# Filling the tile of an FFT with 8 transfers in place of 32, in a kernel that runs attention and a spectral filter side by side

## The chip, the cores and the metric

The kernel runs on one core of a Trainium2 chip. The metric is device time in microseconds, the median of several executions. One profiled execution gives the trace that the profile is read from. TensorE (PE) multiplies, VectorE (DVE), ScalarE (ACT) and GpSimd (POOL) do elementwise work, SyncE (SP) issues transfers; ScalarE and GpSimd issue transfers too, each in the order of its own instructions.

## What is computed

Two independent blocks read inputs of 2048 rows of 448 numbers, and their outputs are joined side by side.

```python
# A: attention of 16 heads of 28, one key head and one value head for all
q = (x @ wq).reshape(B, S, H, Dh).transpose(0, 2, 1, 3)
k, v = x @ wk, x @ wv
p = softmax(einsum("bhqd,bkd->bhqk", q, k) * Dh ** -0.5)
a = einsum("bhqk,bkd->bhqd", p, v).transpose(0, 2, 1, 3).reshape(B, S, H * Dh) @ wo
# B: a two-dimensional real FFT, a complex filter, the inverse
X = rfft2(x, axes=(-2, -1)) * (w_r + 1j * w_i)
b = irfft2(X, s=(S, D), axes=(-2, -1))
return concatenate([a, b], axis=-1)
```

## The kernel before

**The stages.** First come the projections of block A and, between them, the first part of block B's transform: eight loads of `xb` (q = 0 to 7) are folded on VectorE (`fft1_fold`), transformed along the row on TensorE (`fft1_a`) and along part of the column (`fft1_mm`), evicted to the tile `bs` and stored to the DRAM tensor `t1` (`fft1_out`, two stores each, L152). Load q holds the points 2q, 2q + 1, 16 + 2q and 17 + 2q of the 32 that one column index has. Load 7 is finished late, in `first_fill`, after the attention has begun.

**The tile X.** `X` has 128 partitions, 32 points, real and imaginary part, and 113 frequencies. It is filled from `t1` by transfers on GpSimd's queue (`spread`, L486); a partition's run for one point is 112 or 113 numbers. `spread(0)` takes points 0 to 7 and 16 to 23 in 16 transfers, and is called where the attention's schedule begins; `spread(8)` takes the rest in another 16, from `first_fill`. Then VectorE runs a 32-point FFT over X in place (`forward`), multiplies by the filter (`filters`, from tiles `wf` that GpSimd's queue loads, `filter_load`), and runs the inverse (`inverse`), and the result is stored to `t2`. The last part of the inverse (`z_unit`, `y_unit`) is on TensorE again.

A level of the FFT is made of butterflies. `plain` has two instructions (L508, L511) over whole points, 904 elements for four points; `quarter` has four over half points (L520 to L529); a general one has two turns (L550, L552) and two updates (L559, L562). The first level, for m = 16, needs points of both halves: its pairs are points 0 to 3 with 16 to 19, 4 to 7 with 20 to 23, and so on.

**The attention.** There are 16 groups (c, g) of 512 query rows by four heads. For each of 16 blocks of 128 keys, `score` makes four matmuls (L858) into banks of PSUM, and ScalarE takes the exponential of each (L860) into one of 20 buffers `p`. `values` multiplies them by the values and adds in bank 7 (L879), two or three key blocks at a time. After the 16th block `group_out` has VectorE copy bank 7 to SBUF (L755); the next group's values cannot begin until that copy is made. The sums then go through small transfers and a reciprocal (`group_sums`, L765), are spread over the partitions (`R`, L769), and `group_norm` scales the group and splits it in two for the output projection (`w_unit`, L789). `build_q` makes the next group's queries with three VectorE instructions (L170 to L172) and nine transfers on SyncE's queue (L181, L182).

**What sets the order.** TensorE's, VectorE's, ScalarE's and SyncE's instructions are issued in the order in which the Python program calls them; a small model of time (`clk`) decides that order while the program is built. `after(when, dur, f)` puts an event of VectorE at a model time, and `background` holds the FFT's instructions in order, each with a time ahead of which it is not taken. `vector(until)` moves VectorE's model clock on, taking a due event first and else the next background piece. Fill work for TensorE (units `w`, `z`, `y`) is put between scores when it is due. GpSimd's instructions are ordered by the framework's own scheduler. Each engine works strictly in its order, so an instruction that waits holds all that stand behind it. In the model the first level was due at 8.0 (its first two pairs) and at 18.0 (the others).

`first_fill` is called once, after eight scores; it calls `fft1_mm(7)`, `fft1_out(7)`, `spread(8)` and two filter loads. A background piece loads the same two filter tiles again.

Of the kernel before, what the change touches and what calls it, by code (L numbers as in the profile page):

```python
# [37 lines left out]
def kernel(ctx: ExitStack, tc: tile.TileContext, t: dict):  # L38
    nc = tc.nc
# [18 lines left out]
    X = cp.tile([128, 32, 2, 113], F32, name="X")  # L58
    nc.gpsimd.memset(X[64:128, :, :, 112], 0.0)
    t1 = dp.tile([128, 32, DF], F32, name="t1")  # L60
# [69 lines left out]
    def fft1_mm(q):  # L130
        w = xb[q][1]
        pb = view(bank[6], 2, DF), view(bank[7], 2, DF)
        for p in range(2):
            a = at1.pop((q, p))
            for h in range(2):
                for e in range(2):
                    mm(pb[h][64 * e:64 * e + 64, p], w[64 * h:64 * h + 64, 2 * p + e], a[64 * h:64 * h + 64, e],
                       start=True, stop=True)
        return pb

    def fft1_out(q, pb, after=None):
        bs = fp.tile([128, 2, 2, DF], F32, name="bs")
        for h in range(2):
            if q < 6:
                nc.scalar.activation(bs[:, h], pb[h], AF.Copy)
            else:
                ev = nc.vector.tensor_copy(bs[:, h], pb[h])
                if after is not None:
                    behind(ev, after)
        for e in range(2):  # L150
            n0 = 16 * e + 2 * q
            nc.sync.dma_start(t1.rearrange("(l s) n f -> s l n f", l=2)[:, :, n0:n0 + 2], bs[64 * e:64 * e + 64])  # L152
# [33 lines left out]
    with tc.tile_pool(name="f1", bufs=2) as f1[0], tc.tile_pool(name="w1", bufs=1) as w1:  # L186
# [36 lines left out]
        with tc.tile_pool(name="x1", bufs=2) as x1:  # L223
# [102 lines left out]
            for c in range(1, NC):  # L326
                for g in range(NG):
# [22 lines left out]
                    n = 4 * (c - 1) + g  # L350
# [42 lines left out]
        with tc.If(rv > int(np.float32(BOUND).view(np.int32))), tc.tile_pool(name="g1", bufs=1) as g1:  # L393
# [10 lines left out]
            with tc.For_i(0, 64, 1) as n:  # L404
# [3 lines left out]
                for i in range(4):  # L408
                    r = slice(32 * i, 32 * i + 32)
# [31 lines left out]
    clk = {"pe": 0.0, "dve": 4.0, "act": 0.0, "mode": "s", "new": False}  # L441
# [4 lines left out]
    def after(when, dur, f, *a):  # L446
        heapq.heappush(events, (when, next(serial), dur, f, a))
# [14 lines left out]
    def wide(n):  # L462
        return 0.12 + 0.00108 * n
# [10 lines left out]
        nc.gpsimd.tensor_tensor(wol[:, g], w, woh[:, g].bitcast(F32), op=ALU.subtract)  # L474


    t1v = t1.rearrange("(l r k) (e n) f -> l r k e n f", r=2, l=2, e=2)
    Xe = X.rearrange("p (e n) r f -> p e n r f", e=2)

    def spread(n0):  # L480
        for e in range(2):
            for r in range(2):
                for l in range(2):
                    for u, w in ((0, 113), (1, 112)):
                        p = 64 * u + 32 * l
                        nc.gpsimd.dma_start(Xe[p:p + 32, e, n0:n0 + 8, r, :w],  # L486
                                            t1v[l, r][:, e, n0:n0 + 8, 113 * u:113 * u + w])

    spread(0)
    turned = [0] * 32  # L490
    wt = {}
    rows = [slice(0, 113), slice(113, 226)]

    def flat(s):
        return X[:, s].rearrange("p n r f -> p n (r f)")
# [10 lines left out]
    def plain(a, b, n, at=0.0):  # L506
        def first():
            TT(flat(a), flat(a), flat(b), op=ALU.add)  # L508

        def second():  # L510
            STT(flat(b), flat(b), -2.0, flat(a), op0=ALU.mult, op1=ALU.add)  # L511
        for f in first, second:
            background.append((at, wide(226 * n), f))

    def quarter(a, b, n, sign):

        s = float(sign)

        def f0():
            TT(part(a, 0), part(a, 0), part(b, 1), op=ALU.subtract if sign > 0 else ALU.add)  # L520

        def f1():
            TT(part(a, 1), part(a, 1), part(b, 0), op=ALU.add if sign > 0 else ALU.subtract)

        def f2():
            STT(part(b, 0), part(b, 0), -2.0 * s, part(a, 1), op0=ALU.mult, op1=ALU.add)  # L526

        def f3():
            STT(part(b, 1), part(b, 1), 2.0 * s, part(a, 0), op0=ALU.mult, op1=ALU.add)  # L529
            for n in range(*b.indices(32)):  # L530
                turned[n] ^= 1
        for f in f0, f1, f2, f3:
            background.append((0.0, wide(113 * n), f))
# [3 lines left out]
    def turn_by(b, w, k, o, n, new):  # L537

        c, s = w.real / k, w.imag / k

        def go(r):
            def f():
                if r == 0 and new:
                    tw[0] = scratch(4)
                x, y = part(b, r), part(b, 1 - r)
                d = turned[b.start]
                out = tw[0][:, o:o + n, rows[r ^ d]]
                sy = -s if r == 0 else s
                if abs(abs(c) - 1) < 1e-12:
                    STT(out, y, sy, x, op0=ALU.mult, op1=ALU.add if c > 0 else ALU.subtract)  # L550
                else:
                    STT(out, x, c, y, op0=ALU.mult, op1=ALU.add if sy > 0 else ALU.subtract)  # L552
            return f
        for r in range(2):
            background.append((0.0, wide(113 * n), go(r)))

    def update(a, b, o, n, k):
        def f0():
            STT(flat(b), tw[0][:, o:o + n], -k, flat(a), op0=ALU.mult, op1=ALU.add)  # L559

        def f1():
            STT(flat(a), tw[0][:, o:o + n], k, flat(a), op0=ALU.mult, op1=ALU.add)  # L562
        for f in f0, f1:
            background.append((0.0, wide(226 * n), f))

    def big(w):
        return w.real if abs(w.real) >= abs(w.imag) else w.imag

    def cut(a, b, n, step=1):
        for o in range(0, n, 4):  # L570
            m = min(4, n - o)
            yield slice(a + o * step, a + (o + m - 1) * step + 1, step), slice(b + o * step, b + (o + m - 1) * step + 1, step), m

    def forward():
        m, lv = 16, 0
        while m:
            for j in range(16 // m):
                a = 2 * m * j
                w = np.exp(-1j * np.pi * _rev(j, lv) * m / 16)
                for sa, sb, n in cut(a, a + m, m):  # L580
                    if j == 0:
                        plain(sa, sb, n, 8.0 if lv == 0 and sa.start < 8 else 18.0 if lv == 0 else 0.0)
                    elif j == 1:
                        quarter(sa, sb, n, -1)
                    else:
                        k = big(w)
                        turn_by(sb, w, k, 0, n, True)
                        update(sa, sb, 0, n, float(k))
            m, lv = m // 2, lv + 1

    def filter_load(k):
        if k < 8:
            wt[k] = fp.tile([128, 4, 2, 113], F32, name="wf", tag="bs")
            nc.gpsimd.dma_start(wt[k], t["w"][:, 4 * k:4 * k + 4])
# [158 lines left out]
    def group_out(c, g):  # L753
        o = osb[c, g] = qraw[:, g, c * CW:c * CW + CW]
        V.tensor_copy(o, bank[7])  # L755
        taken_out[0] += 1
        sd = dp.tile([4, CW], F32, name="sd", bufs=2)
        rd = dp.tile([4, CW], F32, name="rd", bufs=2)
        rs = ap.tile([128, 16], F32, name="rs")
        nc.gpsimd.dma_start(sd, o[DH::32])  # L760
        nc.gpsimd.dma_start(rs, sd.rearrange("i (a b) -> (i a) b", b=16))
        after(clk["dve"] + 10.0, 0.3, group_sums, c, g, rs, rd)

    def group_sums(c, g, rs, rd):
        V.reciprocal(rs, rs)  # L765
        nc.gpsimd.dma_start(rd.rearrange("i (a b) -> (i a) b", b=16), rs)  # L766
        R = ap.tile([128, CW], F32, name="R", bufs=1)
        for i in range(4):
            nc.gpsimd.dma_start(R[32 * i:32 * i + 32], rd[i:i + 1].to_broadcast([32, CW]))  # L769
        after(clk["dve"] + 10.0, 1.8, group_norm, c, g, R)  # L770

    def group_norm(c, g, R):
        if g == 0:
# [110 lines left out]

    background.append((0.0, 0.0, lambda: [filter_load(k) for k in range(2)]))
    forward()
    for k in range(8):
        filters(k)
    inverse()

    def first_fill():
        pb = fft1_mm(7)
        clk["pe"] += 1.6
        free[6] = inf
        fft1_out(7, pb)
        spread(8)
        for k in range(2):
            filter_load(k)
        clk["dve"] = max(clk["dve"], clk["pe"] + 0.5) + 1.5
        free[6] = clk["dve"] + 0.1  # L900
# [18 lines left out]
    def size():  # L919
        left = 16 - done_steps % 16  # L920
        rich = sum(map(len, work["w"])) * 0.6 + len(work["z"]) * 0.88 > 1.0
        return left if left < 4 else 2 if left == 4 or not rich else 3

    done_steps, quota = 0, 0.0
    n = size()
    while done_steps < 256:
# [9 lines left out]
        elif t_v <= clk["pe"] + 0.05 and (sc >= min(need + LEAD, 1024) or not soon):  # L936
            values(done_steps, n)
            done_steps += n
            n = size()
# [15 lines left out]
        elif t_v <= min(free) or not more:  # L955
            values(done_steps, n)
            done_steps += n
            n = size()
# [11 lines left out]
    c, g = NC - 1, NG - 1  # L970
# [8 lines left out]
    for k in range(4):  # L979
        s = o[:, 128 * k:128 * k + 128]  # L980
        r = ap.tile([128, 128], F32, name="r", bufs=1)
# [18 lines left out]
def _rev(j, bits):  # L1000
    return sum((j >> i & 1) << bits - 1 - i for i in range(bits))
# [109 lines left out]
```

## Time and profile before

| What | us |
|---|---|
| Median of 3 runs | 665.68 |
| The runs | 662.01, 668.57, 665.68 |
| The profiled execution | 661.34 |
| Its span | 659.6 |
| TensorE busy (share of the span) | 636.9 (97%) |
| ScalarE busy | 548.5 (83%) |
| VectorE busy | 329.5 (50%) |
| GpSimd busy | 123.1 (19%) |

Lines name the engine, the line of the kernel and the operation, then the tile written and the tile read by their names in the program. Issues of transfers are rows of the engine whose queue they stand on. "Idle before" is the time for which the engine waited, with what ended the wait. A busy TensorE counts matmuls that overlap, so its share is no measure of its rate.

### The profile page before, as it was taken

The numbers are of one execution on the slowest core, as the hardware profiler recorded it, in microseconds if no ns is written. First come the engines' busy times: TensorE is split into PE (matmuls) and PEld (weight loads), VectorE is DVE, ScalarE is ACT, GpSimd is POOL, SyncE is SP. The second block draws the span as 40 slices with busy tenths as digits, with TensorE's granted clock in tenths as the row PEclk, the third lists the DMA queues.
The fourth block names the chain that finished last, engine by engine and source line by source line (L and its number), as shares of the span: only waits on it lengthen the run. The fifth ranks groups of instructions, "written<-read, shape, count | busy, mean of one in ns | idle before, by whom it ended". The sixth has DMA issues, their size and how long they took to land.

```text
span 659.6 us, 11727 instructions
## 1 busy us (share of the span) xinstructions
PE 636.9 (97%) x4384; PEld 358.6 (54%) x4384; DVE 329.5 (50%) x649; ACT 548.5 (83%) x1101; POOL 123.1 (19%) x219
## 2 busy tenths in 40 slices
PE   9999997399999999999999999999999999999996
PEld 7877543144444445555565655555565556555444
DVE  6999526999999997912143330213043311301013
ACT  5554798199999999898889888898989798889991
POOL 2022375310211111721120302020020101010200
PEclk9999799699999999999999999999999999999999
DMA  8755596112152203992423232041223112120101
GB/s 294 252 153 169 146 222 198 51 46 57 53 164 60 66 18 82 178 201 58 111 102 91 92 98 63 18 116 43 66 89 94 46 33 78 50 63 14 46 1 56
DMA packets 33755, 63.29 MB, mean 96 GB/s; under 512 B 12085, under 2 KB 20710, under 8 KB 32732
## 3 DMA queue, kind: packets, MB, share of 16 engines
q1 hardware_dynamic: 24448, 39.95, 22.8%
q0 software_dynamic: 8672, 21.66, 12.3%
q10 hardware_dynamic: 576, 0.92, 0.4%
q8 instruction: 35, 0.57, 0.3%
q14 instruction: 24, 0.20, 0.1%
HBM read 30.53 MB, written 14.99 MB: 69 GB/s over the span
## 4 chain that ended last, share of the span: by engine, by line
PE 80%; DVE 3%; DMA 3%; SPq 1%; POOL 1%; issue 0%; ACT 0%; ACTq 0%; DVEq 0%; POOLq 0%
PE b L858 36%; PE b L879 34%; PE b L789 6%; PE b L730 2%; PE b L711 2%; DMA qa<-ql 1%; DVE X L508 1%; DMA X<-t 1%; DVE X L511 1%; SPq L181 1%; POOL X L486 1%; DMA ka<-ka 0%; ACT yb L794 0%; SPq L152 0%; DVE X L526 0%
## 5 line engine op out<-in xcount | busy, mean ns | idle before, releaser
L860 ACT ACTIVATE p<-b 128x512 f32<-128x512 f32 x1024 | 507.1, 699 | 66.0 <-PE b L858 66.0
L858 PE MATMUL b<-qa,ka 128*128 128x512 f32 x1024 | 284.8, 411 | 0.4 <-PEq L393 0.4
L879 PE MATMUL b<-p,vs 128*32 128x512 f32 x2048 | 243.5, 600 | 14.9 <-DVE qraw L755 14.9
L858 PEld LDWEIGHTS b<-qa,ka 128*128 128x128 f32 x1024 | 182.6, 189 | 125.7 <-issue 53.3
L879 PEld LDWEIGHTS b<-p,vs 128*32 128x32 f32 x2048 | 55.6, 109 | 140.6 <-issue 124.2
L755 DVE COPY qraw<-b 128x512 f32<-128x512 f32 x15 | 10.4, 691 | 88.5 <-PE b L879 88.5
L760 POOL DMA_DIRECT2D sd<-qraw x15 | 8.8, 589 | 238.8 <-DVE qraw L755 238.8
L797 DVE COPY ya<-b 128x448 f32<-128x448 f32 x12 | 7.5, 625 | 69.3 <-PE b L789 69.3
L769 POOL DMA_DIRECT2D R<-rd x60 | 29.9, 503 | 27.8 <-DMA rd<-rs 27.8
L508 DVE TENSOR_TENSOR X<-X 128x904 f32<-128x904 f32 (+2 forms) x18 | 18.7, 1037 | 19.0 <-DMA X<-t 19.0
L717 DVE COPY X<-b 113x512 f32<-113x512 f32 (+1 forms) x16 | 11.1, 692 | 30.7 <-ACT p L860 21.9
L278 PE MATMUL b<-xh,wqh 128*128 128x512 f32 x64 | 26.0, 406 | 0.0
L278 PE MATMUL b<-xh,wql 128*128 128x512 f32 x64 | 25.1, 391 | 0.1
L777 DVE TENSOR_TENSOR qraw<-qraw,R 128x512 f32<-128x512 f32 x15 | 10.3, 688 | 29.2 <-DMA R<-rd 29.0
L282 ACT ACTIVATE qraw<-b 128x512 f32<-128x512 f32 x16 | 9.2, 599 | 18.5 <-PE b L278 18.5
L735 DVE COPY X<-b 128x226 f32<-128x226 f32 x16 | 6.3, 393 | 36.1 <-ACT p L860 33.9
L766 POOL DMA_DIRECT2D rd<-rs x15 | 8.2, 549 | 80.5 <-DVE rs L765 72.7
L562 DVE SCALAR_TENSOR_TENSOR X<-w,X 128x452 f32<-128x452 f32 (+2 forms) x37 | 21.9, 591 | 1.2
L559 DVE SCALAR_TENSOR_TENSOR X<-w,X 128x452 f32<-128x452 f32 (+2 forms) x37 | 21.9, 591 | 1.2
L789 PE MATMUL b<-woh,oh 128*128 128x448 f32 x60 | 22.0, 367 | 0.0
L789 PE MATMUL b<-wol,oh 128*128 128x448 f32 x60 | 21.9, 365 | 0.0
L789 PE MATMUL b<-woh,ol 128*128 128x448 f32 x60 | 21.9, 365 | 0.0
(106 smaller groups left out, 562.5 us busy)
## 6 DMA issues: line engine op xcount, KB each, us to landing
qa<-qa SPq DMA_DIRECT2D x15, 512.0 KB, 5.2
wf<-w POOLq DMA_DIRECT2D x10, 452.0 KB, 4.3
raw<-xa SPq DMA_DIRECT2D x16, 256.0 KB, 5.4
xb<-xb SPq DMA_DIRECT2D x8, 512.0 KB, 3.6
qa<-qh SPq DMA_DIRECT2D x60, 64.0 KB, 2.0
qa<-ql SPq DMA_DIRECT2D x60, 64.0 KB, 2.0
R<-rd POOLq DMA_DIRECT2D x60, 64.0 KB, 2.2
ob<-X SPq DMA_DIRECT2D x16, 226.0 KB, 2.2
```

The lines of the kernel that those rows point to most:

```text
L278: mm(pq, w[:, j, gs], x[:, j], start=(j == 0 and n == 0), stop=(j == 3 and n == 1))
L508: TT(flat(a), flat(a), flat(b), op=ALU.add)
L559: STT(flat(b), tw[0][:, o:o + n], -k, flat(a), op0=ALU.mult, op1=ALU.add)
L562: STT(flat(a), tw[0][:, o:o + n], k, flat(a), op0=ALU.mult, op1=ALU.add)
L711: mm(pz[:w, j], c2t[q % 2][:, j, o0:o0 + w], fit[q % 2][:, j], start=True, stop=True)
L717: V.tensor_copy(zt[q % 2][e][:w], view(bank[b], 4, 128)[:w].rearrange("p j (r n) -> p r j n", r=2))
L730: mm(py[:, k], z[:w, r, js], fc["cs3"][:w, k], start=True, stop=True)
L769: nc.gpsimd.dma_start(R[32 * i:32 * i + 32], rd[i:i + 1].to_broadcast([32, CW]))
L789: mm(p, x[c][:, g, s], w[:, g], start=(g == 0 and n == 0), stop=(g == NG - 1 and n == 2))
L858: mm(bank[b], ka[:, kc * 128:(kc + 1) * 128], qa[c, g][:, h], start=True, stop=True)
L860: nc.scalar.activation(p, bank[b], AF.Exp, scale=SCALE)
L879: mm(bank[7][32 * i:32 * i + 32], vs[:, kc], pt.pop(4 * st + i), start=(kc == 0), stop=(kc == 15))
```

## The change

X is filled by eight transfers, one for each real or imaginary part, half of the rows and half of the frequencies, with all 32 points. They are issued in `first_fill`; the earlier call is gone. The first level of the FFT is due at 22.0 in the model, all four pairs alike, and a group's norm 12 after its sums in place of 10. Shapes, durations in the model and everything else stay.

```diff
-    t1v = t1.rearrange("(l r k) (e n) f -> l r k e n f", r=2, l=2, e=2)
-    Xe = X.rearrange("p (e n) r f -> p e n r f", e=2)
-
-    def spread(n0):
-        for e in range(2):
-            for r in range(2):
-                for l in range(2):
-                    for u, w in ((0, 113), (1, 112)):
-                        p = 64 * u + 32 * l
-                        nc.gpsimd.dma_start(Xe[p:p + 32, e, n0:n0 + 8, r, :w],
-                                            t1v[l, r][:, e, n0:n0 + 8, 113 * u:113 * u + w])
-
-    spread(0)
+    t1v = t1.rearrange("(l r k) n f -> l r k n f", r=2, l=2)
+
+    def spread():
+        for r in range(2):
+            for l in range(2):
+                for u, w in ((0, 113), (1, 112)):
+                    p = 64 * u + 32 * l
+                    nc.gpsimd.dma_start(X[p:p + 32, :, r, :w], t1v[l, r][:, :, 113 * u:113 * u + w])
+
...
-                        plain(sa, sb, n, 8.0 if lv == 0 and sa.start < 8 else 18.0 if lv == 0 else 0.0)
+                        plain(sa, sb, n, 22.0 if lv == 0 else 0.0)
...
-        after(clk["dve"] + 10.0, 1.8, group_norm, c, g, R)
+        after(clk["dve"] + 12.0, 1.8, group_norm, c, g, R)
...
-        spread(8)
+        spread()
```

The changed program has four lines fewer from `spread` on, so that the copy L755 is its L751.

## The prediction

> **What bounds the kernel now.** I read the page first (span, chain, groups), then the timeline around the one long wait that it names, then the DMA views of the time ahead of that wait.
>
> ```profile
> span 659.6 us, 11727 instructions
> ...
> PE 80%; DVE 3%; DMA 3%; SPq 1%; POOL 1%; issue 0%; ACT 0%; ACTq 0%; DVEq 0%; POOLq 0%
> ...
> L879 PE MATMUL b<-p,vs 128*32 128x512 f32 x2048 | 243.5, 600 | 14.9 <-DVE qraw L755 14.9
> ```
>
> The chain that ended last is TensorE for 80% of the span, and TensorE has one large idle stretch: 14.9 us ahead of a value product (L879), ended by VectorE's copy of the bank of values (L755, in `group_out`). The table of stages shows the rest (columns: stretch, its length, busy time of PE, PEld, DVE, ACT, POOL, granted clock, DMA share, GB/s):
>
> ```profile
> 78.00:80.00 2.00, 2.00 (x14) 0.99 (x16) 1.93 (x5) 1.86 (x4) 0.28 (x1) 1.00 0.02 4
> 96.00:98.00 2.00, 2.00 (x14) 1.05 (x6) 1.78 (x2) 2.00 (x5) 2.00 (x5) 1.00 0.99 211
> 98.00:100.00 2.00, 2.00 (x16) 0.79 (x18) 0.00 (x0) 2.00 (x5) 0.90 (x2) 1.00 1.03 223
> 102.00:104.00 2.00, 2.00 (x16) 0.70 (x18) 0.06 (x1) 2.00 (x5) 0.32 (x1) 1.00 1.02 302
> 132.00:165.00 33.00, 33.00 (x205) 15.66 (x198) 31.76 (x80) 33.00 (x69) 3.69 (x7) 1.00 0.21 50
> ```
>
> From 132 us on TensorE and ScalarE are busy all the time and VectorE nearly so. So the change must show in the stall, or make a new one. TensorE's part of the timeline of the stall (start, length, engine, line):
>
> ```profile
> 108.47 2.12 PE L858 MATMUL b<-qa,ka 128*128 128x512 f32 x8
> 125.52 3.32 PE L879 MATMUL b<-p,vs 128*32 128x512 f32 x16 [14.93 <-DVE qraw L755]
> ```
>
> VectorE's part:
>
> ```profile
> 103.94 1.10 DVE L508 TENSOR_TENSOR X<-X 128x904 f32<-128x904 f32 x1 [6.13 <-DMA X<-t]
> ...
> 118.71 0.62 DVE L520 TENSOR_TENSOR X<-X 128x452 f32<-128x452 f32 x1
> ...
> 120.99 1.09 DVE L508 TENSOR_TENSOR X<-X 128x904 f32<-128x904 f32 x1
> ...
> 123.13 0.54 DVE L170 TENSOR_SCALAR qt<-qraw,mask,cvec 128x512 f32<-128x512 f32 x1
> ...
> 124.78 0.68 DVE L755 COPY qraw<-b 128x512 f32<-128x512 f32 x1
> ```
>
> GpSimd's groups between 103 and 126 us:
>
> ```profile
> L474 POOL TENSOR_TENSOR wol<-wo,woh 128x448 fp32r<-128x448 f32 x3 | 4.2, 1400 | 0.2
> L473 POOL CAST woh<-wo 128x448 fp32r<-128x448 f32 x4 | 3.6, 902 | 1.7 <-DMA wo<-wo 1.6
> ```
>
> TensorE ends its last score at 108.47 + 2.12 = 110.6 and has nothing left that it may do. The copy could be made by then, but VectorE works in order, and ahead of the copy stand 18 butterflies that cannot start before the last transfer into X lands at 103.9. TensorE's restart is thus the landing of X plus VectorE's work from there to the copy. A stall of this kind stays after the change; its length moves.
>
> **The change part by part.** *VectorE's order.* As built, the changed program has nine butterflies of 904 elements, the three instructions of the next queries (L170 to L172), then the copy. Before, it was 18 after the landing (ten of 904 elements, eight of 452), and four more ahead of it. Nine at 1.10 us are 9.9 us. The three query instructions take 124.78 - 123.13 = 1.65, and from the copy's start to TensorE's restart 125.52 - 124.78 = 0.74 pass. VectorE also runs slower beside GpSimd's casts of wo: 103.94 to 123.13 is 19.2 us, while ten at 1.10 and eight at 0.57 (four in 118.71 to 120.99) are 15.6. The 3.6 us of excess fall to the three L474 and four L473 of that time, about 1.0 for a pair. In the changed order two of the four pairs come while VectorE waits; the loads of the last two are queued behind X and land just after it: 2.0 us. So restart = landing + 9.9 + 2.0 + 1.65 + 0.74 = landing + 14.3 (before: 125.52 - 103.94 = 21.6). With no collision it is 12.3, with four 16.3.
>
> *The fill.* Here the change loses. GpSimd's queue:
>
> ```profile
> 68.69 2.31 POOL L486 DMA_DIRECT2D X<-t  x4 [2.35 <-DVE qa L163]
> ...
> 80.27 5.33 POOL L486 DMA_DIRECT2D X<-t  x9
> ```
>
> The chain, where it passes the stores of t1 and the last transfer into X:
>
> ```profile
> 73.65 1.11 SPq L152
> ...
> 98.31 5.61 DMA X<-t
> ```
>
> DMA issues (KB each, median us to landing), and then min/median/max of the landing of the filter loads:
>
> ```profile
> qa<-qa SPq DMA_DIRECT2D x15, 512.0 KB, 5.2
> wf<-w POOLq DMA_DIRECT2D x10, 452.0 KB, 4.3
> qa<-qh SPq DMA_DIRECT2D x60, 64.0 KB, 2.0
> t<-bs SPq DMA_DIRECT2D x16, 225.0 KB, 4.2
> X<-t POOLq DMA_DIRECT2D x16, 113.0 KB, 5.6
> X<-t POOLq DMA_DIRECT2D x16, 112.0 KB, 5.6
> cs<-cs POOLq DMA_DIRECT2D x1, 199.5 KB, 4.3
> ```
>
> ```profile
> DMA to landing us min/median/max: 3.4/4.3/4.8
> ```
>
> Before, six of the 32 transfers were issued by 71 us, and 26 from 80.27 on. After, all eight need the last stores of t1, so none goes early, and on GpSimd's queue three loads of filters stand ahead of them, each into the buffer of the one before, so that each waits for the landing of the last. The first needs the stores issued from 73.65; the DMA share of 0.02 after 78 says that they had landed by then. So the first filter load goes out at 77.7 and lands 3.4 later (81.1); the second, beside other traffic, 4.6 later (85.7); the third is issued then, and X starts at 86.3. Issuing costs nothing that counts: 2.31 us for four.
>
> What follows is bytes. X is 16 x 113 + 16 x 112 KB = 3600 KB in both versions, in runs of 113 numbers. With the third filter load (452) and the copy of the queries (512) 4.67 MB are queued. While X fills the queue, at 96 to 100 us, 217 GB/s move at a share near 1: 21.5 us. The same working for before: 26 transfers (2925 KB), 2 x 225, 512, eight of 64 and 199.5 KB from 80.27 on are 4.71 MB, 21.7 us, so 102.0; it landed at 98.31 + 5.61 = 103.92, 1.9 later. With that 1.9 the new landing is 86.3 + 21.5 + 1.9 = 109.7. Bounds: at the 302 GB/s of 102 to 104 us, where filter rows flow, 15.5 us and a landing at 103.7; at the whole pace of before, 26 transfers in 23.65 us or 0.91 for 113 KB, 29.1 us and 115.4. I take the middle, since its rate was measured on runs of the same length.
>
> The restart is then 109.7 + 14.3 = 124.0, against 125.52: 1.5 us gained.
>
> [...]
>
> *What moves behind the copy.* Before, VectorE reached the second copy without a wait and the third with 0.96 us to spare:
>
> ```profile
> 156.25 0.68 DVE L755 COPY qraw<-b 128x512 f32<-128x512 f32 x1
> 187.56 0.69 DVE L755 COPY qraw<-b 128x512 f32<-128x512 f32 x1 [0.96 <-PE b L879]
> ```
>
> ```profile
> L735 DVE COPY X<-b 128x226 f32<-128x226 f32 x16 | 6.3, 393 | 36.1 <-ACT p L860 33.9
> ```
>
> TensorE's group between them takes 31.3 us, and VectorE needed 30.35 of it. Changed, seven butterflies of 904 elements, 24 of 452, eleven of 226 (0.39 each, as L735), a norm (three instructions, as the queries), the queries and a copy lie between the first copy and the second: 7.7 + 13.7 + 4.3 + 1.65 + 1.65 + 0.7 = 29.7 us; to the third the mix is the one that took 30.35. Both are under 31.3, so this costs nothing; TensorE's scores and values hide it. If that cover is gone, each us over is a us of stall in that group.
>
> *The norms,* due after 12 in place of 10, cost nothing either: TensorE's order as built has the same 68 double and 40 triple value steps; the first output projection stands 8 scores later and the first inverse transform 40, which is the room that a later filter stage needs. Uncovered, a late norm would stop a projection by as much as it is late.
>
> *Sum:* 661.34 (the profiled execution, 1.7 around its span) - 1.5 = 659.8. That execution lies 4.3 below the median of the runs, 665.68; on the median's scale the sum is 664.2.
>
> **The rivals.** *A, the large transfers flow faster:* at 302 GB/s X lands at 103.7, restart 118.0, 7.5 gained: 658.2; without collisions 9.5: 656.2. For it: few transfers, four of them issued at once. Against: the queue was already full (share 1.03) at 223 GB/s. [...]
>
> *B, the fill is late (slower):* begun at 86.3 instead of 65, it moves at the whole pace of before, 0.91, lands at 115.4, restart 129.7, 4.2 lost: 669.9; with all four pairs of casts colliding 6.2 lost: 671.9. It decides from a landing of 111.2 on (125.5 - 14.3). For it: six early transfers are lost and three chained loads gained. Against: that pace has 512 KB of small query copies in it, which now go ahead.
>
> *C, VectorE falls behind at a later copy:* there are 1 to 1.6 us of room in a group; if the counts are 3 us short in two groups, some 3 are lost after the gain of 1.5: 667. Against: VectorE's work in all is unchanged.
>
> **How the numbers follow.** Forecast 0.53, A 0.22, B 0.18, C 0.07. One per cent, about what a measurement of this kernel can tell from no change, is 6.7 us. A crosses it mostly (0.17), the forecast by the spread of the runs to either side (0.05), B in its late half (0.11) and C at times (0.02): faster 0.22, same 0.60, slower 0.18. The likeliest case alone spans landings from 106.5 to 113: 661 to 668. The range reaches to A without collisions and to B with them: 656.5 to 671.5.
>
> **What would show it.** Right: the first transfer into X issued at 86 to 87 behind three filter loads; X landing at 107 to 112, with 210 to 220 GB/s ahead of it; nine butterflies, then the copy; a wait of 11 to 16 us before the value product; no other wait of TensorE over 1 us. Wrong: rates near 300 GB/s (A), a landing past 112 (B), TensorE waiting at the second to sixth copy (C), or filter loads that are not chained, which would start X near 82 and bring 4 us more.

## The result and the profile after

The changed kernel takes 669.90 us, the median of 20 runs, beside 666.08 for the kernel before in 20 runs of the same set: a ratio of 1.0062, 95% interval 1.0044 to 1.0079. It is slower by 0.6%; a gain of 1.5 us was forecast. The profiled execution took 671.82 us.

Lines of the changed kernel are four lower than before from the fill on: L875 is the value product L879, L751 the copy L755, L504 and L507 the butterflies L508 and L511. From the page and its groups by line:

```profile
span 670.1 us, 11703 instructions
...
L875 PE MATMUL b<-p,vs 128*32 128x512 f32 x2048 | 243.8, 601 | 25.5 <-DVE qraw L751 25.5
```

TensorE still has one long wait, at the same place, and it is 25.5 us in place of 14.9. The difference, 10.6, is the difference of the two profiled spans, 10.5. GpSimd's queue in the timeline (start, length, what was issued, the wait ahead of it):

```profile
78.89 0.57 POOL L590 DMA_DIRECT2D wf<-w  x1 [13.19 <-DVE qt L170]
85.12 0.55 POOL L590 DMA_DIRECT2D wf<-w  x1 [5.66 <-DMA wf<-w]
86.52 0.55 POOL L468 DMA_DIRECT2D cs<-cs  x1 [0.85 <-DMA qa<-ql]
87.06 1.07 POOL L472 DMA_DIRECT2D wo<-wo  x2
90.47 0.54 POOL L590 DMA_DIRECT2D wf<-w  x1 [2.35 <-DMA qa<-ql]
91.13 6.26 POOL L484 DMA_DIRECT2D X<-t  x8
```

VectorE's part of the timeline, from the landing of X to TensorE's restart:

```profile
119.17 1.10 DVE L504 TENSOR_TENSOR X<-X 128x904 f32<-128x904 f32 x1 [39.10 <-DMA wo<-wo]
...
122.80 1.91 DVE L507 SCALAR_TENSOR_TENSOR X<-X 128x904 f32<-128x904 f32 x1
...
132.23 1.09 DVE L504 TENSOR_TENSOR X<-X 128x904 f32<-128x904 f32 x1
133.24 0.54 DVE L170 TENSOR_SCALAR qt<-qraw,mask,cvec 128x512 f32<-128x512 f32 x1
...
134.89 0.68 DVE L751 COPY qraw<-b 128x512 f32<-128x512 f32 x1
```

And TensorE's:

```profile
108.00 2.11 PE L854 MATMUL b<-qa,ka 128*128 128x512 f32 x8
135.62 3.64 PE L875 MATMUL b<-p,vs 128*32 128x512 f32 x16 [25.52 <-DVE qraw L751]
```

X is issued at 91.13 and lands at 119.17 (before: 103.94); landing here and below is the start of the first butterfly that had to wait for it. The first VectorE line names a load of `wo` as what ended the wait. That load stands behind X on the queue; the last transfer into X, issued at 96.6, itself landed 22.2 us later, at 118.8. Eleven butterflies follow, the three query instructions, the copy, and TensorE restarts at 135.62: 16.45 after the landing (before: 21.58). So the landing costs 15.2 and the order gives 5.1 back, 10.1 in all. Only 3.8 of that is in the medians, and where the rest went is settled below by a second profile of the kernel before.

The stage table ahead of the landing (columns as before: stretch, its length, five engines' busy time, granted clock, DMA share, GB/s):

```profile
104.00:112.00 8.00, 6.11 (x36) 3.26 (x32) 0.00 (x0) 7.84 (x17) 1.02 (x2) 1.00 1.06 190
```

X alone is in flight there, as the packets suggest: 409 hold 1.52 MB, the same mean as from 97 to 100 us, ahead of the loads issued at 100.3 to 105.2 (148 hold 0.55), and from 116 to 119 us 182 hold 0.79. The DMA engines are as busy as before (share 1.06) and carry 190 GB/s, where 223 to 228 flowed at 98 to 102 us of the kernel before, whose second row is:

```profile
100.00:102.00 2.00, 2.00 (x14) 1.14 (x7) 0.00 (x0) 2.00 (x5) 1.34 (x3) 1.00 1.08 228
```

### The profile page after: what moved, and what is told of

The parts are those of the page before. It is cut to its first block, busy times and chain, and to the rows that moved or that the text cites. A ratio compares the mean times of both kernels' runs of the same rounds, so it can differ in the third digit from the quotient of the medians.

```text
span 670.1 us, 11703 instructions
## 1 busy us (share of the span) xinstructions
PE 636.8 (95%) x4384; PEld 358.2 (53%) x4384; DVE 325.4 (49%) x649; ACT 548.8 (82%) x1101; POOL 111.4 (17%) x195
## 4 chain that ended last, share of the span: by engine, by line
PE 89%; DMA 3%; ACT 3%; DVE 2%; issue 0%; POOL 0%; SPq 0%; ACTq 0%; DVEq 0%; POOLq 0%
PE b L854 37%; PE b L875 33%; PE b L278 6%; PE b L785 5%; ACT p L856 3%; DMA wo<-wo 2%; PE b L726 2%; PE b L707 2%; PE b L122 2%; PE b L137 1%; DVE X L504 1%; DVE X L507 1%; DMA raw<-wq 1%; ACT yb L790 0%; POOL wol L474 0%
## 5 line engine op out<-in xcount | busy, mean ns | idle before, releaser
L875 PE MATMUL b<-p,vs 128*32 128x512 f32 x2048 | 243.8, 601 | 25.5 <-DVE qraw L751 25.5
L875 PEld LDWEIGHTS b<-p,vs 128*32 128x32 f32 x2048 | 55.6, 109 | 152.2 <-issue 125.2
L751 DVE COPY qraw<-b 128x512 f32<-128x512 f32 x15 | 10.4, 691 | 67.4 <-PE b L875 67.4
L504 DVE TENSOR_TENSOR X<-X 128x904 f32<-128x904 f32 (+2 forms) x18 | 18.0, 1002 | 39.1 <-DMA wo<-wo 39.1
L762 POOL DMA_DIRECT2D rd<-rs x15 | 8.2, 545 | 87.1 <-DVE rs L761 79.7
L555 DVE SCALAR_TENSOR_TENSOR X<-w,X 128x452 f32<-128x452 f32 (+2 forms) x37 | 21.8, 589 | 1.1
L507 DVE SCALAR_TENSOR_TENSOR X<-X 128x904 f32<-128x904 f32 (+2 forms) x18 | 19.0, 1056 | 0.5
```

Of the source, the lines that this page charges most:

```text
L875: mm(bank[7][32 * i:32 * i + 32], vs[:, kc], pt.pop(4 * st + i), start=(kc == 0), stop=(kc == 15))
```

## The experiments

The theory after this comparison: **the new fill loses, by a late landing, and the new due times gain, by fewer butterflies ahead of the copy.** The rivals: the order or the norms cost time; the fill's loss is the size of its transfers; the loss lies elsewhere. Ratios are against the kernel before on the same chip, with 95% intervals; the kernel before took 661.3 us (median) on the chip of e5 to e8 and 664 to 667 on all others.

**The change in two parts.** e1 keeps the 32 transfers and takes the due times alone:

```diff
-  plain(sa, sb, n, 8.0 if lv == 0 and sa.start < 8 else 18.0 if lv == 0 else 0.0)
+  plain(sa, sb, n, 22.0 if lv == 0 else 0.0)
-  after(clk["dve"] + 10.0, 1.8, group_norm, c, g, R)
+  after(clk["dve"] + 12.0, 1.8, group_norm, c, g, R)
```

> The fill of before (32 transfers), with the changed due times alone (first level 22, norms 12). Theory 1 (the late landing is the whole loss; the new order by itself is a gain): X lands at 103.9 us as before, the copy of values follows after eleven butterflies in place of 18, TensorE restarts 16.5 later, at about 120.4 in place of 125.5; the stall falls from 14.9 to about 10, and the time by about 5 us, ratio 0.992. Rival (the new order or the later norms cost time, at later copies or at TensorE's order): slower than before, ratio about 1.006, with TensorE waits at the second to sixth copy.

Measured: 652.32 us, ratio 0.9786 (0.9763 to 0.9810), almost three times the expected gain. VectorE's timeline of e1:

```profile
93.44 1.10 DVE L508 TENSOR_TENSOR X<-X 128x904 f32<-128x904 f32 x1 [12.66 <-DMA X<-t]
...
96.72 1.10 DVE L511 SCALAR_TENSOR_TENSOR X<-X 128x904 f32<-128x904 f32 x1
103.86 1.10 DVE L508 TENSOR_TENSOR X<-X 128x904 f32<-128x904 f32 x1 [6.04 <-DMA X<-t]
...
115.32 0.68 DVE L755 COPY qraw<-b 128x512 f32<-128x512 f32 x1
```

With the old fill the first half of X is in at 93.4, so four of the eleven butterflies are done ahead of the landing and only seven stand between it and the copy: 11.5 us from landing to copy, 15.7 in the changed kernel. The stall is 5.2 us. So the new fill takes more than its lateness: it also takes away the early half.

e2 is the reverse: the 8 transfers of the change with the due times 8, 18 and 10 of before (the diff above, taken back).

> The changed fill (8 transfers) with the due times of before (8 and 18, norms 10). Theory 1: X starts at about 91 and lands at about 119 as in the changed kernel, and the copy still stands behind all first-level butterflies of the groups, 22 to 26 us of VectorE's work: restart at about 141 to 145, a stall of 30 to 35 us, time 13 to 20 us longer, ratio 1.02 to 1.03. Rival (the fill is harmless, the order makes the loss): ratio 1.00, landing near 104.

Measured: 683.38 us, ratio 1.0244 (1.0204 to 1.0285). From VectorE's timeline of e2:

```profile
117.27 1.10 DVE L504 TENSOR_TENSOR X<-X 128x904 f32<-128x904 f32 x1 [38.08 <-DMA wo<-wo]
...
140.83 0.68 DVE L751 COPY qraw<-b 128x512 f32<-128x512 f32 x1
```

X lands at 117.27, the copy follows at 140.83, the stall is 32.3. The rival is out: the fill by itself is a loss of 18 us. The groups of e2 show a second wait that the theory had not named; it comes back below:

```profile
L854 PE MATMUL b<-qa,ka 128*128 128x512 f32 x1024 | 285.6, 411 | 3.3 <-DVE X L713 2.9 <-DVE bs L147 0.4
```

e12 repeats e1 and e11 the changed kernel, on one chip.

> The changed kernel once more, so that the runs beside it have it on their own chip. Theory 1: X starts at 90 to 91, lands at 118 to 119, TensorE waits 24 to 26 us at the first copy, ratio 1.006. Rival (its loss belongs to the chip on which it was measured): ratio 1.000 or less.

> The old fill with the changed due times once more, beside the changed kernel. Theory 1 (the new order is the gain, the new fill the loss): ratio 0.979 here as on the other chip, 2.5% under the changed kernel; stall 5 us. Rival (the earlier 2.1% was of that chip): ratio 0.986, the 9.5 us by which the restart moved in the profile.

Measured: the changed kernel 670.50, ratio 1.0061 (1.0037 to 1.0085); e12 652.28, ratio 0.9776 (0.9731 to 0.9821). In e11 X starts at 88.8 and lands at 116.05, the copy stands at 131.77; in e12 the landing is at 103.47 and the copy at 114.93. Of the 16.84 us between the copies 12.58 are the landing and 4.26 the four butterflies that no longer precede it. The times differ by 18.2. e11's stall, 21.8, fell short of the expected 24 to 26: the landing moves by some 3 us between executions (119.17 in the first profile, 116.05 here).

**Which number, level or norm?** e16 changes the first level's due time alone, e8 and (on another chip) e17 the norms' alone: one of the two lines of e1's diff each.

> Before with the first level due at 22 and the norms left at 10. Theory 1 (the first level's place is the whole gain: 9.5 us at the first copy and, since the output's inverse transform comes later, no copy of its bank behind the reciprocal that waits for a trip through memory, the 2 us wait of the second profile of before): stall 5 us, no second wait, as with both numbers changed, ratio 0.977 to 0.980 where before takes 666, 0.986 where it takes 661. Rival (the norms' 12 is what takes the second wait away): the second wait of 2 us returns in the profile or in the time, ratio 0.984 where before takes 666.

> Before with the groups' norms due after 12 in place of 10, nothing else. By the step of the prediction that costs the norms at nothing: stall at the first copy unchanged (restart 21.6 after the landing), no other wait, ratio 1.000 within 0.003. Rival (the norms are part of the change's loss or gain: they stand on VectorE's way to the next copies or hold up an output projection): ratio off by 0.004 or more to either side, with the place in TensorE's waits.

> Before with the norms due at 12 alone, once more. Theory 1: level with before on any chip, ratio 1.000 within 0.003, and the copy of the inverse transform's bank still right behind the reciprocal. Rival: 0.994 where before takes 666, since the second wait goes.

Measured: level alone 652.11, ratio 0.9805 (0.9782 to 0.9829), stall 5.7; norms alone 0.9988 (0.9976 to 1.0000) and 1.0012 (0.9988 to 1.0036). The level is the whole gain, the norms are nothing.

**Where 6 us went between profile and median.** e13 is the kernel before, unchanged, for a second profile, with the changed kernel (e14) beside it on the same chip.

> The kernel before, unchanged, for a second profile of it. Its first profile (661.34 us, restart of TensorE at 125.5) lies below nearly all its runs on three chips (medians 666.1, 665.7, 666.7) and at the median of one (661.3). Theory 1 (where it takes 666, X lands later or VectorE takes longer to the copy): a stall of 18 to 20 us in place of 14.9, restart at 129 to 130, and the rest as in the first profile. Rival (the difference lies elsewhere, spread over the run as a lower clock or in a second wait): stall 15, and 4 to 5 us more in other waits or in TensorE's busy time.

> The changed kernel beside it on the same chip. Theory 1: its stall is as much longer than that of the kernel before in the same set as its time, 4 us for a ratio of 1.006, landing 116 to 119. Rival: the stalls differ by 10 us as in the first two profiles while the times differ by 4, so something gives 6 us back behind the stall.

Measured: e13 664.50, 0.9979 (0.9954 to 1.0003); e14 669.28, 1.0069 (1.0052 to 1.0087). The theory in e13 fell: its first stall is 14.6, no longer than in the first profile. The rival holds, with a second wait. TensorE's waits in e13:

```profile
PE b L879 <- DVE qraw L755: 14.6, 1, 14.6
PE b L858 <- DVE X L717: 2.0, 1, 2.0
```

VectorE's timeline there, in e13:

```profile
303.39 0.25 DVE L765 RECIPROCAL rs<-rs 128x16 f32<-128x16 f32 x1 [7.59 <-DMA rs<-sd]
303.99 0.69 DVE L717 COPY X<-b 113x512 f32<-113x512 f32 x1 [0.34 <-ACT p L860]
```

and in the first profile of before:

```profile
300.99 0.25 DVE L765 RECIPROCAL rs<-rs 128x16 f32<-128x16 f32 x1 [4.36 <-DMA rs<-sd]
302.12 0.69 DVE L717 COPY X<-b 113x512 f32<-113x512 f32 x1 [0.88 <-ACT p L860]
```

The copy L717 empties a bank of the output's inverse transform, and stands in VectorE's order behind the reciprocal of a group's sums, which waits for two transfers through memory. When these take longer, as in e13 (the reciprocal's wait is 7.59 us there, 4.36 in the first profile), TensorE waits 2.0 us for the bank. TensorE's timeline in e13 after it, and a row of the stage table, whose third number from the end is the granted clock, the share of full speed at which TensorE was let run:

```profile
304.73 0.91 PE L858 MATMUL b<-qa,ka 128*128 128x512 f32 x2 [2.00 <-DVE X L717]
305.57 4.24 PE L879 MATMUL b<-p,vs 128*32 128x512 f32 x24
```

```profile
306.00:308.00 2.00, 2.00 (x12) 0.40 (x8) 0.00 (x0) 0.36 (x1) 1.87 (x4) 0.50 0.22 72
```

At a granted clock of 0.50 the next 24 value products take 4.24 us, 2.78 elsewhere in the trace. Wait and slow restart together are 3.5 us. e17 shows the same in its profiled execution of 665.68 us: a wait of 2.3 for L717, and 4.48 for the 24 products. The 2.9 us of e2 are the same wait: there too the copy stands right behind the reciprocal. In the profiles of the changed kernel, of e1 and of e16 no copy L717 stands there, since with the first level later the inverse transform comes later; none has this wait. So the change does gain behind the stall: from e13 to e14 the restart moves by 9.05 us (124.54 to 133.59) and the span by 4.2; the rest of the run, from the restart on, is 4.9 shorter, 3.5 of it this wait and its restart. All traces with a long first wait agree: from TensorE's restart to the end of the span the twelve without this second wait take 533.3 to 535.2 us, the three with it (e13, e17, e2) 538.2 to 539.4, in the mean 4.3 more. That the executions of before near 666 all have this wait is inferred from these two and from the two near 661 (the first profile and e8) that lack it. Why the trip through memory is longer in some executions stays open.

**What makes the landing late.** e3 takes the two filter loads out of `first_fill`, so that one stands ahead of X (the background loads these tiles in any case):

```diff
-    background.append((0.0, 0.0, lambda: [filter_load(k) for k in range(2)]))
+    background.append((22.0, 0.0, lambda: [filter_load(k) for k in range(2)]))
         spread()
-        for k in range(2):
-            filter_load(k)
```

> The changed kernel, with the two filter loads that stand ahead of the fill taken out (their rows are loaded again by the background, whose start moves to 22), so that one filter load in place of three is ahead of X on GpSimd's queue. Theory 1 (start of X counts as much as its rate): X starts at about 84 to 85 in place of 91.1, lands at about 112 to 113, TensorE restarts at about 129, stall about 19, about 6 us faster than the changed kernel and level with before, ratio 1.00. Rival (the queue is full whatever the start, only bytes count): the landing moves by the 0.9 MB of the two loads at most, some 3 us or less, ratio 1.002 to 1.006.

Measured: 666.06, ratio 0.9999 (0.9979 to 1.0020). GpSimd's queue in e3:

```profile
78.73 0.57 POOL L590 DMA_DIRECT2D wf<-w  x1 [13.16 <-DMA ka<-ka]
...
87.12 6.26 POOL L484 DMA_DIRECT2D X<-t  x8 [4.83 <-DMA qa<-qh]
```

X starts at 87.12 and lands at 114.06, 2 to 5 us ahead of the changed kernel's three profiles. The chain of loads is part of the loss, but without it X still starts only at 87.1: all eight transfers need the two last stores of `t1`, issued at 79.7 and 80.3 here. (The line names a later transfer on the same queue of SyncE; when the two stores landed, no view of e3 shows.)

Then the transfers themselves. e5 cuts each of the eight into four of 113 KB that take every second of 16 points; e9 and e10 take 8 neighbouring points as before did, all held back by an order of issue until the last stores are in. In e9 consecutive transfers go round the four groups of 32 partitions, as before; in e10 (and e5) four in a row write the same 32.

```diff
+        for n0, r, l, u, w in [(n0, r, l, u, w) for n0 in (8, 24, 0, 16) for r in range(2) for l in range(2) for u, w in ((0, 113), (1, 112))]:
+            p = 64 * u + 32 * l
+            d = nc.gpsimd.dma_start(X[p:p + 32, n0:n0 + 8, r, :w],
+                                    t1v[l, r][:, n0:n0 + 8, 113 * u:113 * u + w])
+            if first is None:
+                first = d
+            else:
+                behind(d, first)
```

These are e9's lines; in e10 `for n0 in (8, 24, 0, 16)` stands last in the list, so that it runs fastest.

> The changed kernel with each of its 8 transfers cut into four that take every second of 16 points: 32 transfers of 113 or 112 KB again, in the same runs of 113 numbers and the same place on the queues, but each still needs all stores, as the 8 do. Theory 1 (large transfers carry less: X alone moved at 182 to 196 GB/s in the changed kernel and in the one without the filter loads, at 223 to 228 in small transfers before): from 99 us on 17 us in place of 20, X lands at about 116 in place of 119, TensorE restarts at about 132.5, 3 us faster than the changed kernel, ratio 1.002. Rival 1 (the rate belongs to the runs, whatever the size of a transfer, and the loss is the late start alone): landing 119, ratio 1.006. Rival 2 (issuing limits: 32 times 0.58 us on GpSimd, 18.6 us, after a start at 91): last issue at 110, landing 116 to 117 at a DMA share below 1.

> The changed kernel with 32 transfers of 8 neighbouring points, as before, in an order that goes round the partitions as before's does, but all held on GpSimd's queue until the last stores are in, behind the same three filter loads. Size, run length and neighbourhood are those of before, start and place on the queue those of the changed kernel. Theory 1 (the rate of 223 to 228 GB/s in before's last small transfers belongs to their shape): X alone moves at 220 or more, landing at about 116, restart 132.5, ratio 1.002 (other things equal). Rival (no shape makes it: X alone moves at about 187 whenever it starts as one late block): 181 to 195 GB/s, landing at 119, ratio 1.006.

> The same 32 late transfers of 8 neighbouring points, with the four of one group of 32 partitions one after the other, as in the run with every second point. Theory 1 (what slows is several transfers into the same partitions at a time, which large transfers and this order share): X alone at 181 to 195 GB/s here while the order that goes round the partitions has 220. Rival (the steps between points make the rate): 220 here too.

Measured: e5 667.45, ratio 1.0097 (1.0078 to 1.0117) where before takes 661.3; e9 666.19, 0.9996 (0.9969 to 1.0023); e10 668.29, 1.0020 (1.0000 to 1.0040). As built, the third filter load stands behind X in all three, not ahead as expected, so X starts earlier than in the changed kernel (88.5, 85.9 and 87.8) and the times alone prove little. The rates do. One row of the stage table each, from 102 to 110 us, of e5, e9 and e10 in this order:

```profile
102.00:110.00 8.00, 7.70 (x48) 3.52 (x40) 0.00 (x0) 7.84 (x17) 7.20 (x14) 1.00 1.05 187
```

```profile
102.00:110.00 8.00, 8.00 (x50) 3.83 (x49) 0.00 (x0) 7.84 (x17) 7.96 (x15) 1.00 0.88 202
```

```profile
102.00:110.00 8.00, 7.86 (x49) 3.64 (x48) 0.00 (x0) 7.84 (x18) 7.26 (x13) 1.00 1.02 187
```

e9 and e10 differ in nothing but the order of the same 32 transfers. Round the partitions they carry 202 GB/s with the DMA engines busy 0.88 of the time, 230 for each busy share; four in a row into the same partitions carry 187 at 1.02. The size made no difference here: 187 in e5 and e10, 190 in the large ones. e9 does not reach 220: from 101.36 us on GpSimd issues 14 transfers without a pause, in 8.04 us, and 0.58 us for 113 KB is an estimated 200 GB/s. Its landing, 112.75, comes hardly sooner after its start (26.8 us) than e11's (27.2). So in this kernel the faster order is worth little once the start is late. And e9, with transfers of the size and the order of before, still lands 8.8 us later than before, and 3 to 6 us ahead of the changed kernel, whose X starts 3 to 5 us after e9's: the larger part of the late landing is the late start.

**Taking the copy out of the way.** If the copy's place is all, it can stand ahead of the butterflies. e4 is before with the first level due at 36; e7 the changed kernel with 48.

> Before with one number changed: the first level's due time is 36 for all pairs, so that the first copy of values stands ahead of all butterflies in VectorE's order. Theory 1 (the stall is nothing but the copy's place behind butterflies that wait for X): the copy runs right after TensorE's last score, at about 111, and the stall shrinks from 14.9 to 1 us or less; 13 to 15 us faster, ratio 0.977 to 0.980, unless the butterflies do not fit into the next groups. Rival (the 22 displaced butterflies, some 22 us of VectorE's work, come due in groups where VectorE has 1 to 2 us of room in 31.3): TensorE waits at the second to sixth copy for as much as it gained at the first, ratio 0.995 to 1.00.

> The changed kernel with the first level's due time 48, so that the first copy of values stands ahead of all butterflies, with the 8 late transfers kept. Theory 1 (the late landing costs only through the copy that waits behind it): no stall at the first copy, X still lands at about 119, VectorE idles from 111 to 119 and has 20 us of work before the second copy at about 142: done by 140, no stall there. What is left is VectorE's backlog at the output transform: 4 us in the run with the old fill and all butterflies behind, here up to 8 more: 652 to 660, ratio 0.980 to 0.99. Rival (the landing costs by itself, whatever the order): as the changed kernel, 670, ratio 1.006.

Measured: e4 653.20, ratio 0.9808 (0.9783 to 0.9832); e7 654.39, 0.9905 (0.9878 to 0.9932), 1.6 points better than the changed kernel on the other chips though X starts as late (at 88.81, in e11 at 88.82). Neither waits at the first copy. What is left stands further back: in e4 4.2 us ahead of a product of the inverse transform (L711), in e7 3.2 at the copy behind the reciprocal, and 1.5 and 1.7 at the second copy. TensorE's waits in e4, then in e7:

```profile
PE b L711 <- DMA sd<-qraw: 4.2, 1, 4.2
PE b L879 <- DVE qraw L755: 1.5, 1, 1.5
```

```profile
PE b L854 <- DVE X L713: 3.2, 1, 3.2
PE b L875 <- DVE qraw L751: 1.7, 1, 1.7
```

e6 and (on another chip) e15 put only what is ready ahead of the copy: the four butterflies of the early half.

```diff
-  plain(sa, sb, n, 8.0 if lv == 0 and sa.start < 8 else 18.0 if lv == 0 else 0.0)
+  plain(sa, sb, n, 22.0 if lv == 0 and sa.start < 8 else 36.0 if lv == 0 else 0.0)
```

> Before with two numbers changed: the first level's due times are 22 for the pairs of the first half of each points' list, whose data land at about 93, and 36 for the rest, so that four butterflies stand ahead of the first copy, in VectorE's idle time before the landing at 104, and all others behind it. Theory 1 (a copy ahead of what waits for X takes the stall away, and the wait of 4.2 us in the output transform of the run with all butterflies behind the copy comes from VectorE's backlog): no stall at the first copy, at most 1 at the second, the wait of 4.2 gone: 648 to 650 us, ratio 0.973 to 0.976. Rival (the backlog of 18 butterflies still shows): 652 to 653, as the run with all behind, ratio 0.980.

> The old fill, due times 22 and 36, once more beside both. Theory 1 (no stall is left to vary): 645 to 648 us whatever the chip, so the ratio follows the kernel before: 0.970 where that takes 666, 0.978 where it takes 661. Rival (the ratio is the chip's): 0.978 again.

Measured: 646.41, ratio 0.9782 (0.9762 to 0.9801), and 646.24, ratio 0.9721 (0.9701 to 0.9741). This version, with the 32 transfers, beats both kernels: 2.2 to 2.8% under before, 23 us under the changed one on e15's chip. Its time is the same on both chips while that of before differs by 4, as the second wait has it. TensorE's waits in e15:

```profile
PE b L879 <- DVE qraw L755: 1.2, 1, 1.2
PE b L137 <- ACT bs L145: 1.1, 1, 1.1
```

## Why the prediction was wrong

**What bounds the kernel, and the form of the sum: right.** The restart is the landing of X plus VectorE's work up to the copy; e1, e2, e4 and e7 each move it as that says. The rival that came true is B, the late fill, by its condition, a landing past 111.2. That its 669.9 is the measured median to the tenth is luck: B has the restart at 129.7 and 4.2 us lost, while the three profiles of the changed kernel have it at 132.5 to 135.6, and a wait behind the stall, which B does not know, goes the other way. The same two errors, partly against each other, keep the measured time inside the stated range.

**The start of X: 86.3 forecast, 91.13 in the first profile** (88.8 and 90.0 in two others). The first filter load went out at 78.89, not 77.7, and the first two took 6.2 and 5.4 us to the issue of the next (in e11 4.2 and 5.6), not 3.4 and 4.6: 1.2 and 3.6 us. A reading failed as well: the stores of `t1` were taken as landed by 78 from a DMA share of 0.02, but two more are issued at 78.4 and 79.1 in the changed kernel (78.9 on in before), beside the first filter load. In the changed kernel the loads end last; in e3, with one load ahead of X, its wait of 4.83 us, up to 87.1, is put down to the stores.

**The bytes behind it: 21.5 + 1.9 us forecast, 28.0 measured.** The rate failed. The 217 GB/s were the mean of two rows, 211 and 223, taken as measured on runs of X's length. In the row at 211 (96 to 98 us of before) the copy of the queries on SyncE's queue moved 0.37 of the 0.42 MB. Only that at 223 is X's, and it belongs to small transfers going round the partitions; the eight large ones carried 190. For X's 3.69 MB that is an estimated 2.4 us. The other 2.2 are not settled. In the 28.0 us some 5.6 MB moved, where 4.67 were counted: the loads behind X on the queue, issued at 100.3 to 105.2, were nearly in when its last transfer landed. Whether they held it up, no run here shows. (`cs` and two loads of `wo` ahead of X were not counted either, but had landed by 92.0.) The bound from the whole pace of before, 29.1 us, came nearer than the middle that was taken.

**VectorE's order: nine butterflies forecast, eleven found;** the count was wrong. Landing to restart was put at 14.3 and was 16.45, the two extra ones at 1.1 us each; the two collisions with casts, 2.0, are there as said (1.45 and 1.91 us for 1.10, twice, beside GpSimd's L473 and L474 from 120.39 to 127.07).

These three are 4.8 + 4.6 + 2.15 = 11.6, the distance of the restart, 135.6, from the forecast 124.0.

**The four butterflies ahead of the landing** were named, for before, but that the new fill loses their cover was given no price: 4.3 us, by e11 and e12.

**Later copies and norms: right for the changed kernel.** No later copy stalls, and e8 and e17 put the norms at nothing. But the prediction looked for waits that the change might add behind the stall, on the evidence of one profile, and not for one that it might take away. That step was incomplete by 3.5 us in TensorE's trace, in executions that the first profile does not stand for, and it is why a restart 9 to 10 us later cost only 3.8. It is also what the sum's last step had wrong: the 4.3 us added to go from the profiled execution to the median's scale are, as far as these traces tell, this wait, which before has and the changed kernel has not.

## What to carry to other kernels

Fewer and larger transfers gave away two things that the timeline of the old fill shows: an early half, on which work could start, and an early place on the queue; each of the eight had to wait for the last stores of `t1`. Where an in-order engine has a copy that another engine waits for, put ahead of it only what is ready by then: one due time brought 13 us here, and a split of it some 6 more (652 to 646), with no transfer touched. And one profile is one execution: a wait that is there only when a trip through memory runs late (7.59 us for 4.36 here) must be looked for in a second one.

## What the runs showed of the hardware that was not expected

The order of equal transfers over the partitions changed their rate: 202 GB/s at a DMA share of 0.88 going round the four groups of 32, 187 at 1.02 with four in a row into one group (e9, e10). Why, no run here shows.

In e13 and in the changed kernel a wait cost more than its length. After the wait of 2.0 us in e13 the granted clock was 0.50 and 24 products took 4.24 us for 2.78; after the stall of 25.5 us in the changed kernel it was 0.50 from 136 to 138 us, and 16 took 3.64 for 1.92, so 1.5 and 1.7 us came on top of these waits. But in e6, after a wait of 1.96 us at the second copy, 16 products took 1.92. What decides between these cases no run here shows.
